# The second tile's k halves on two engines, and a new order of the first output rows, in an attention plus MoE kernel

## Chip, cores and metric

One core of a Trainium2 chip. The metric is the device time of one execution in microseconds (us), lower is better. Engines are named as in the profile: PE is TensorE (PEld its weight loads), ACT ScalarE, DVE VectorE, POOL GpSimd, SP SyncE, which issues all DMAs of the kernel before but two 64 KB stores.

## The reference

Chunked softmax attention (8 sequences, 8 heads, 576 positions, chunks of 64) feeds a two-layer MLP with exact GELU. Float32 in and out; the kernel works in bf16.

```python
# attention inside chunks of 64
scores = scale * np.matmul(q_c, k_c.transpose(0, 1, 2, 4, 3))
attn = softmax(scores)
out = np.matmul(attn, v_c)
# MLP on 4608 tokens
x = out.transpose(0, 2, 1, 3).reshape(4608, 512)
h = x @ w_in                                 # 512 -> 2048
g = 0.5 * h * (1.0 + erf(h / sqrt(2)))
y = g @ w_out                                # 2048 -> 512
```

## The kernel before

Nine tiles of 512 tokens. For each, `mm1` (x by w_in, then GELU) and `mm2` (h by w_out) keep TensorE busy, and the attention of the *next* tile is laced in between. The change is in `phase(0)`: while mm2 of the first tile runs by rows of w_out (twelve rows of four matmuls, one for each output block of 128 tokens), q and k of the second tile are transposed on TensorE, copied out of PSUM, and used.

```python
def transposed(t, nm, g):
    pool, tag = (ps_tp, "tp") if t or nm == "q" else (ps_mm, "mm")   # ps_tp has 2 banks
    tp = pool.tile([P, 2, J, P], bf16, tag=tag, name="tp")
    for j in range(J):
        nc.tensor.transpose(tp[:, 0, j], tiles[t][nm][:, g, j]..., ident[:])
    return ...

def att_Tk(t, g, copy):
    tp = transposed(t, "k", g)
    for r in range(2):                      # partitions 0-63, then 64-127
        sl = slice(CH * r, CH * (r + 1))
        copy(k_bds[g][sl, :, sl]..., tp[sl])

def mm2_rows(t, f):
    for ms in range(MT // P):
        if f == 0:
            pool, tag = (ps_at, "at") if ms == 3 else (ps_mm, "mm")   # ps_mm: 3 banks, shared with mm1
            tiles[t]["y_ps", ms] = pool.tile(...)
        nc.tensor.matmul(tiles[t]["y_ps", ms][:], h[:, f, ms * P:(ms + 1) * P], w_out_sb[:, f, :], ...)

phase(0, {}, {0: [lambda: act_table(Act.Exp)],
              2: [T[0]], 3: [T[2]], 4: [T[4], T[6]], 7: [T[1], T[3]], 8: [T[5], S_[0]],
              9: [T[7], S_[1], next_qk], 10: [S_[2], att_sum, cast of w_out row 14 by DVE],
              11: [cast of w_out row 15 by ACT, S_[3]], 12: [sums], 13: [A[0], ...], ...}, by_rows=True)
```

T[0], T[2], T[4], T[6] are the q transposes of groups 0 to 3; T[1], T[3], T[5], T[7] those of k. S_ are score matmuls, A the products with v. The k copies of groups 0 and 1 are ScalarE's, those of 2 and 3 VectorE's.

The softmax here doesn't subtract the row's maximum and nothing guards it: scores larger than these inputs give would overflow.

## Time and profile before

| | before |
|---|---|
| time, median of 4 | 290.65 us (290.45 to 291.22) |
| span in the profile | 288.9 us |
| PE busy | 278.2 us (96%) |
| first mm2 matmul of the first tile | 31.72 us |
| from there to the end | 257.1 us |

PE is busy all but about 11 us. The prediction below shows the two gaps that the change aims at. The records of the transpose bank (durations as least/median/most ns, first and last start in us) give the price of a half copy on either engine:

```profile
L157 ACT COPY k_bd<-tp x4: 578/579/580, 39.5 to 41.3; 64x512 bf16<-64x512 bf16 x4
L157 DVE COPY k_bd<-tp x4: 683/688/695, 41.1 to 43.3; 64x512 bf16<-64x512 bf16 x4
```

And GpSimd's timeline (start, duration, line, work, count, and in brackets the idle time before it and what ended that) shows the casts that feed TensorE in this stretch: w_out rows 8 to 11, then rows 12 and 13, then v of the second tile.

```profile
39.64 2.29 POOL L432 CAST w_out_sb<-arrival 128x512 bf16<-128x512 f32 x4 [0.94 <-DMA arrival<-in_moe_w_out_dram]
43.15 1.17 POOL L432 CAST w_out_sb<-arrival 128x512 bf16<-128x512 f32 x2 [1.22 <-DMA arrival<-in_moe_w_out_dram]
44.27 5.38 POOL L137 CAST v_bd<-arrival 64x512 bf16<-64x512 f32 x8
```

The first two of these lines start when a load lands; the v casts follow the second at once. So this stretch is fed by the DMA stream, with about 1 us to spare: row 8's cast, the first of the four, ends at about 39.64 + 0.61 = 40.25 us, and its matmuls start at 41.17.

### The profile page before, as it was taken

What the parts mean: (1) busy time and instruction counts of PE and PEld (TensorE: products, weight loads), DVE (VectorE), ACT (ScalarE), POOL (GpSimd) and SP (SyncE); (2) the same over time, 40 slices, a digit from 0 to 9 for tenths busy, and PEclk for the clock granted to TensorE, in tenths of its full rate; (3) what the DMA queues carried; (4) which work ended last, traced back from release to release, by engine and by line L of the source; (5) the groups of instructions that cost most, each with busy time, mean ns of one, the idle gap of its engine ahead of it and who ended that gap; (6) DMA issues with size and microseconds to landing.
All of it is one profiled execution on the core that took longest, in us unless ns stands there. A gap on an engine that the chain in (4) does not pass through costs nothing.

```text
span 288.9 us, 4859 instructions
## 1 busy us (share of the span) xinstructions
PE 278.2 (96%) x1836; PEld 138.5 (48%) x1870; DVE 154.8 (54%) x265; ACT 170.1 (59%) x329; POOL 98.8 (34%) x136
## 2 busy tenths in 40 slices
PE   7699999999999999999999999999999999999994
PEld 2454455445544554455445544554455445544444
DVE  6854349348805882749246935394268425850011
ACT  3767766967447844785468536763785368626400
POOL 6859758605651830262008400650003610000000
PEclk9999999999999999999999999999999999999999
DMA  6999999999799726961698259914999970120033
GB/s 222 247 360 404 393 337 265 254 207 286 191 291 311 168 99 161 325 145 74 161 261 234 76 138 285 233 73 115 163 130 131 265 147 2 39 106 2 0 73 73
DMA packets 96887, 53.79 MB, mean 186 GB/s; under 512 B 68576, under 2 KB 89312, under 8 KB 96864
## 3 DMA queue, kind: packets, MB, share of 16 engines
q1 hardware_dynamic: 96704, 53.36, 69.8%
q8 instruction: 14, 0.23, 0.3%
q10 hardware_dynamic: 160, 0.13, 0.2%
q14 instruction: 9, 0.07, 0.1%
HBM read 36.70 MB, written 9.44 MB: 160 GB/s over the span
## 4 chain that ended last, share of the span: by engine, by line
PE 90%; DVE 3%; ACT 3%; DMA 2%; issue 1%; SPq 0%; POOL 0%; DVEq 0%; POOLq 0%
PE h_ps L328 42%; PE y_ps L344 37%; PE av_ps L289 3%; PE y_ps L384 3%; PE s_ps L180 2%; DMA arrival<-in_k_dram 2%; ACT k_bd L157 2%; PE y_ps L369 1%; DVE x L296 1%; PE tp L144 1%; PE rc_ps L276 1%; DVE rc L259 1%; ACT pT L194 1%; SPq L112 0%; PE s_ps L192 0%
## 5 line engine op out<-in xcount | busy, mean ns | idle before, releaser
L328 PE MATMUL h_ps<-x,w_in_sb 128*128 128x512 bf16 x565 | 125.8, 379 | 1.0 <-DVE x L296 0.4
L331 ACT ACTIVATE h<-h_ps 128x512 bf16<-128x512 f32 x144 | 85.5, 597 | 62.5 <-PE h_ps L328 62.4
L344 PE MATMUL y_ps<-w_out_sb,h 128*128 128x512 bf16 x493 | 117.9, 379 | 0.9
L328 PEld LDWEIGHTS <-w_in_sb 128*128 128x128 bf16 x576 | 56.2, 98 | 68.4 <-issue 1.2
L344 PEld LDWEIGHTS <-h 128*128 128x128 bf16 x512 | 46.0, 98 | 46.5 <-issue 0.2
L172 DVE COPY k_bd<-k_t 64x512 bf16<-64x512 bf16 x56 | 35.6, 636 | 53.6 <-DMA k_t<-k_nat 52.6
L133 POOL CAST q_nat<-arrival 128x512 bf16<-128x512 f32 x31 | 21.2, 720 | 95.0 <-DMA arrival<-in_q_dram 95.0
L137 POOL CAST v_bd<-arrival 64x512 bf16<-64x512 f32 (+1 forms) x30 | 36.3, 1210 | 20.5 <-DMA arrival<-in_v_dram 13.3
L296 DVE TENSOR_TENSOR x<-av_ps,rc 128x512 bf16<-128x512 f32 x36 | 24.8, 692 | 4.7 <-PE av_ps L289 1.4
L133 POOL CAST k_nat<-arrival 128x512 bf16<-128x512 f32 x34 | 20.1, 625 | 11.2 <-DMA arrival<-in_k_dram 9.2
L448 ACT ACT_TABLE_LOAD x18 | 23.1, 1283 | 1.0 <-PEq L587 0.7
L353 DVE COPY y_sb<-y_ps 128x512 f32<-128x512 f32 x11 | 7.6, 691 | 29.7 <-PE y_ps L344 27.8
L353 ACT COPY y_sb<-y_ps 128x512 f32<-128x512 f32 x24 | 13.8, 580 | 14.7 <-PE y_ps L344 14.4
L239 DVE STREAM_TRANSPOSE pt<-pT 128x256 f32<-128x256 f32 x28 | 12.2, 437 | 18.8 <-ACT pT L183 18.8
L259 DVE STREAM_TRANSPOSE rc<-rb 128x512 f32<-128x512 f32 x31 | 21.5, 692 | 0.2 <-ACT rb L229 0.2
L242 DVE TENSOR_REDUCE part<-pt 128x16 f32<-128x512 bf16 x28 | 19.2, 686 | 1.0
L250 ACT COPY other<-part 32x32 f32<-32x32 f32 x56 | 12.0, 215 | 10.4 <-DVE part L242 9.9
L289 PEld LDWEIGHTS <-v_bd 128*128 128x128 bf16 x288 | 13.0, 98 | 8.0 <-issue 0.3
L183 ACT ACTIVATE pT<-s_ps 128x512 bf16<-128x512 f32 x28 | 14.7, 590 | 0.0
L289 PE MATMUL av_ps<-pT,v_bd 128*128 128x64 bf16 x288 | 14.3, 193 | 0.2
L180 PEld LDWEIGHTS <-k_bd 128*128 128x128 bf16 x224 | 10.4, 98 | 6.6
L384 PE MATMUL y_ps<-w_out_sb,h 128*128 128x512 bf16 x46 | 11.9, 379 | 0.4 <-ACT h L331 0.3
(68 smaller groups left out, 136.5 us busy)
## 6 DMA issues: line engine op xcount, KB each, us to landing
arrival<-in_v_dram SPq DMA_DIRECT2D x72, 128.0 KB, 4.1
out_dram<-y_sb SPq DMA_DIRECT2D x32, 256.0 KB, 2.3
arrival<-in_q_dram SPq DMA_DIRECT2D x7, 1024.0 KB, 6.7
arrival<-in_k_dram SPq DMA_DIRECT2D x7, 1024.0 KB, 9.1
arrival<-in_moe_w_out_dram SPq DMA_DIRECT2D x4, 1024.0 KB, 12.2
arrival<-in_moe_w_in_dram SPq DMA_DIRECT2D x4, 512.0 KB, 6.2
arrival<-in_moe_w_in_dram SPq DMA_DIRECT2D x2, 1024.0 KB, 10.4
arrival<-in_q_dram SPq DMA_DIRECT2D x4, 256.0 KB, 4.7
```

What stands on the lines that cost most here:

```text
L133: copy(st[nm][:, g].rearrange("p j r d -> p r j d"), st[nm + "f"][:, 2 * g:2 * g + 2])
L137: copy(v_bds[t % NV][sl, :, gs, sl].rearrange("p i g d -> p g i d"), tiles[t]["vf"][sl, gs])
L172: copy(k_bds[g][sl, :, sl].rearrange("p i (c j) -> p i c j", j=J), src[sl])
L259: nc.vector.transpose(rc[:], src.to_broadcast([P, NB, 32]))
L289: nc.tensor.matmul(av_ps[:, i, :], v_bds[t % NV][:, i, g, :], st["pT", g][:, i, :], start=True, stop=True)
L296: nc.vector.tensor_tensor(x, av, rc, op=mybir.AluOpType.mult)
L328: nc.tensor.matmul(h_ps[a][:], w_in_sb[:, ks, (f + a) * P:(f + a + 1) * P], st["x"][:, ks, :], start=(ks == 0), stop=(ks == KS - 1))
L331: nc.scalar.activation(st["h"][:, f + a, :], h_ps[a][:], Act.Gelu)
L344: nc.tensor.matmul(y_ps[:], st["h"][:, f, ms * P:(ms + 1) * P], w_out_sb[:, f, :], start=(f == 0), stop=(f == FF - 1))
L353: (AC if ms < 3 and t + 1 < NT else DV)(y_sb[:], y_ps[:])
L384: nc.tensor.matmul(tiles[t]["y_ps", ms][:], tiles[t]["h"][:, f, ms * P:(ms + 1) * P], w_out_sb[:, f, :], start=(f == 0), stop=False)
L448: nc.scalar.activation(act_scratch[:], rest[:, 0:1], func)
```

## The change

The intent: free a transpose bank sooner, by giving ScalarE the lower and VectorE the upper half of each k group of the second tile, and let the first mm2 rows begin with block 3, which has a bank of the attention pool, so that block 2, whose bank waits for the last GELU (to 32.52 us in the trace before), comes only after row 1 has started.

```diff
-    def att_Tk(t, g, copy):
+    def att_Tk(t, g, copies):
         tp = transposed(t, "k", g)
         for r in range(2):
             sl = slice(CH * r, CH * (r + 1))
-            copy(k_bds[g][sl, :, sl]..., tp[sl])
+            copies[r](k_bds[g][sl, :, sl]..., tp[sl])
...
-            T += [..., lambda g=g: att_Tk(t, g, ck if t == 0 or g < 2 else DV)]
+            T += [..., lambda g=g: att_Tk(t, g, (ck, ck if t == 0 else DV))]
...
     def mm2_rows(t, f):
-        for ms in range(MT // P):
+        todo = [(f, ms) for ms in (3, 0, 1, 2)]
+        if f < 2:
+            todo = [(f, ms) for ms in (3, 0, 1)] if f == 0 else [(1, 3), (1, 0), (1, 1), (0, 2), (1, 2)]
+        for f, ms in todo:
```

`...` stands for unchanged lines and rearrangements of axes.

More of the change, by code (lines that the diff above doesn't have):

```diff
@@ L156, in att_Tk @@
             sl = slice(CH * r, CH * (r + 1))
-            copy(k_bds[g][sl, :, sl].rearrange("p i (c j) -> p i c j", j=J), tp[sl])
+            copies[r](k_bds[g][sl, :, sl].rearrange("p i (c j) -> p i c j", j=J), tp[sl])
     def flip(t, nm):
@@ L304, in att_units @@
         for g in range(G):
-            T += [lambda g=g: att_Tq(t, g, cq), lambda g=g: att_Tk(t, g, ck if t == 0 or g < 2 else DV)]
+            T += [lambda g=g: att_Tq(t, g, cq), lambda g=g: att_Tk(t, g, (ck, ck if t == 0 else DV))]
         S_ = [lambda g=g: att_S(t, g) for g in range(G)]
```

## The prediction

> **What bounds the kernel now.** I read the page first, then TensorE's waits, then the chain of work that ended last and the timeline for the one stretch that the change touches (31 to 53 us: mm2 of the first tile, with the attention of the second tile laced into it).
>
> The page's first part and the by-line part of its chain:
> ```profile
> PE 278.2 (96%) x1836; PEld 138.5 (48%) x1870; DVE 154.8 (54%) x265; ACT 170.1 (59%) x329; POOL 98.8 (34%) x136
> ...
> PE 90%; DVE 3%; ACT 3%; DMA 2%; issue 1%; SPq 0%; POOL 0%; DVEq 0%; POOLq 0%
> ```
> TensorE is 96% busy and 90% of the chain. So only its gaps can be won, and only those that other work does not re-open later. TensorE's waits in the window 31 to 53 us (total, times, longest) are:
> ```profile
> PE y_ps L384 <- ACT h L331: 0.3, 1, 0.3
> PE h_ps L328 <- DVE x L296: 0.2, 1, 0.2
> PE tp L144 <- ACT k_bd L157: 0.2, 1, 0.2
> ```
> The change aims at the first and the third. The listed sizes are too small, because a matmul's record runs on to its modelled end (379 ns) while the next starts 216 ns after it (the chain shows 0.86 us for every four). From the timeline of TensorE (start, duration, line, count):
> ```profile
> 31.72 0.59 PE L384 MATMUL y_ps<-w_out_sb,h 128*128 128x512 bf16 x2
> 32.57 1.46 PE L384 MATMUL y_ps<-w_out_sb,h 128*128 128x512 bf16 x6 [0.25 <-ACT h L331]
> ...
> 39.07 0.61 PE L144 MATMUL tp<-ident,k_nat 128*128 128x128 bf16 x8
> 39.52 1.03 PE L384 MATMUL y_ps<-w_out_sb,h 128*128 128x512 bf16 x4
> 40.72 0.38 PE L144 MATMUL tp<-ident,k_nat 128*128 128x128 bf16 x4 [0.17 <-ACT k_bd L157]
> ```
> First gap: two matmuls from 31.72 leave TensorE free at 31.72 + 2 x 0.216 = 32.15, and the third starts at 32.57: **0.42 us**. The third is output block 2 of the first row. It takes the bank that the last GELU reads, and that GELU ends at 32.52. Second gap: four matmuls from 39.52 end their slots at 40.38, and the third group's k transposes start at 40.72: **0.34 us**. They wait for the first of two transpose banks, which ScalarE empties in two copies in a row:
> ```profile
> 39.50 0.58 ACT k_bd L157
> 40.08 0.01 issue
> 40.09 0.59 ACT k_bd L157
> 40.68 0.04 issue
> 40.72 0.38 PE tp L144 x4
> ...
> 44.01 0.73 DVE t L204
> ...
> 52.12 0.70 DVE x L296
> ```
> (the chain in order of time.) From 44.01 to 52.82 the chain leaves TensorE: VectorE's sums, reciprocals and x products with four small ScalarE copies, each starting where the one before ended. It ends with x of the fourth group and a wait of 52.87 - (51.23 + 6 x 0.216) = 0.34 us at the head of the next tile's mm1. The change does not shorten that chain, so what counts is whether its first link moves. It does: before 44.01 the chain shows the column-sum matmul on TensorE (to 43.98), while VectorE had been free since 43.95.
>
> [...] The halves here are partitions 0 to 63 and 64 to 127[...]. This trace has no two engines in one bank at once[...]. [...] The trace has 688 and 579 ns; I use those. [...] GpSimd's w_out casts take 614 ns beside VectorE's k copies, and 834 to 868 ns beside VectorE's casts from SBUF. [...]
>
> **The change part by part.**
>
> 1. Output-block order. The number of matmuls stays at 48 in these rows. Row 0 now issues blocks 3, 0, 1 (block 3 has a bank of the attention pool, free since the first tile), row 1 issues 3, 0, 1, and only then come block 2 of rows 0 and 1. Six matmuls from 31.72 end their slots at 33.02, half a microsecond after the GELU's end at 32.52. All eight run without a gap to 33.45; before, they ended at 33.86. Gain **0.41 us**, if nothing up to the next part waits. ScalarE's table load (32.54 to 33.82) and its small activation (to 34.03) stay put. The first qT copy can start at 34.03 instead of 34.29, so it gains only 0.26, but its bank is next wanted some 1.6 us later. The k casts (VectorE and GpSimd) end by 38.71. The first two groups' casts end near 37.9, and the moved k transposes start at 38.65. No new wait.
>
> 2. Halves on two engines. The eight half copies stay eight, still four by ScalarE (579 ns) and four by VectorE (688 ns). They are divided by half instead of by group. With part 1 in, the transposes of groups 0 and 1 start at 38.65 and the first bank is full at 39.08. ScalarE's half ends at 39.66, VectorE's at 39.77, the bank is free at about 39.81. VectorE was idle from 38.24 to 41.14 before, so it costs nothing there. TensorE wants the bank at 39.10 + 0.864 = 39.97. So the second gap goes: **0.34 us**, with 0.15 us in hand. Group 1's bank is free at about 40.5 and wanted at 41.27. The k blocks are ready for the score matmuls as well.
>
> Sum: 0.41 + 0.34 = **0.75 us** by the time of the column sum, which then ends near 43.23. VectorE has finished its last k half by about 42.4, so its chain starts 0.75 us earlier with all links unchanged. The w_out block that VectorE casts inside the chain landed by 43.15, and it moves from 45.76 to 45.01: no DMA wait. The 0.34 us wait for x at the end stays.
>
> What follows must keep it. The second tile's successors hang on DMA that does not move: k_bd copies at 61.73 to 66.69, score matmuls from 64.74 at 1.1 us each. The tightest margin there is over 1 us. GpSimd's v casts run 66.83 + 3.84 = 70.67, wanted at 71.71, after the change at 70.96: 0.29 us left, the tightest place of all. Later tiles repeat every 29.5 us, which is TensorE's own work, so the gain travels to the end. 290.73 - 0.75 = 289.98, say **290.0 us**, 0.26% faster.
>
> **The rivals.** First, **the halves serialise**, by a dependency on the shared bank or k block or by slower access. Group 0's bank would then be free at about 39.08 + 0.58 + 0.04 + 0.69 + 0.04 = 40.43, and TensorE would wait 0.46 us in place of 0.34. Only about 0.3 us of the gain is left: 290.4. Against it: [...]the w_in and w_out casts show that different engines fill slices of one tile at once. Second, **a DMA-fed cast takes over**. The w_out row for slot 8 is cast by GpSimd from 39.64, when its load lands, to about 40.25. TensorE now wants it at 40.41. With 0.15 us in hand, a load that lands 0.3 us late gives back some 0.15 us: 290.1. The same holds for v at 70.67; a loss of all the gain there needs about 1 us of delay: 290.7. Third, **VectorE becomes the bound** because it holds k halves of all four groups. Its work is the same 2.8 us and is done earlier, so I give this little weight. If the last half came late it would delay the chain at 43.23 only after 0.8 us of slack. Fourth, the parts lean on each other: if only part 1 held, 290.3; if only part 2, 290.4.
>
> **Range and chances.** 0.75 us is about the spread of the three runs before (290.45 to 291.22), so noise of some 0.4 us either way weighs as much as the mechanism. I take 289.5 to 290.7: the low end is the sum plus noise, the high end the gain given back. Faster by 2% would need 5.8 us, and the whole stretch has some 1.2 us of TensorE gaps. Slower by 2% would need a new wait in every tile, and only this stretch changes. Faster 0.01, within 2% 0.98, slower 0.01.
>
> **What would show it right or wrong.** Right: no gap among the first eight y_ps matmuls of L384's successor; q transposes 0.41 us earlier; k half copies of ScalarE and VectorE starting within 0.05 us of each other at about 39.1, at 579 and 688 ns; no wait of the third k transposes on either; the column sum's transpose on VectorE near 43.25; the mm1 of tile 2 some 0.75 us earlier, and the span near 288.15. The wait for x of about 0.34 us is still there. Wrong: VectorE's half starting after ScalarE's, longer copies, a TensorE wait on w_out or v casts, or an early lead that is gone by the third tile's mm2.

## The result, and the profile after

Ratios in this document are the mean time of one kernel's fast runs over that of the other's in the same rounds, so not quite the ratio of the medians quoted.

| | before | changed |
|---|---|---|
| time, median | 290.65 us (4 runs) | 291.19 us (290.62 to 291.44, 4 runs) |
| ratio | | 1.0013, 95% interval 0.9992 to 1.0033 |
| predicted | | 290.0 us, range 289.5 to 290.7 |

The measured time is outside the range, on the slow side. Yet the two profiled spans are equal, 288.9 us.

In the changed kernel's timeline of TensorE, the eight matmuls of the first two rows now run without a gap. But the third k transposes start at 40.75, not when the four matmuls from 39.42 end their slots (39.42 + 0.86 = 40.28):

```profile
32.03 1.89 PE L387 MATMUL y_ps<-w_out_sb,h 128*128 128x512 bf16 x8
...
38.97 0.61 PE L144 MATMUL tp<-ident,k_nat 128*128 128x128 bf16 x8
39.42 1.03 PE L387 MATMUL y_ps<-w_out_sb,h 128*128 128x512 bf16 x4
40.75 0.38 PE L144 MATMUL tp<-ident,k_nat 128*128 128x128 bf16 x4 [0.31 <-DVE k_bd L157]
```

That is a gap of 0.47 us where the kernel before had 0.34. The waits of TensorE's matmuls in 30 to 54 us have one line left, and it names VectorE. Its weight loads, which are listed apart (PEld), wait once for the third group's v, which delays the matmuls by 0.03 us; the kernel before has no such line:

```profile
PE tp L144 <- DVE k_bd L157: 0.3, 1, 0.3
...
PEld L289 <- POOL v_bd L137: 0.4, 1, 0.4
```

The chain in order of time says why:

```profile
39.39 0.59 ACT k_bd L157
39.98 0.02 issue
40.01 0.71 DVE k_bd L157
40.71 0.04 issue
40.75 0.38 PE tp L144 x4
...
45.96 0.41 PE sums_ps L218 x4
46.37 0.02 issue
46.40 0.73 DVE t L221
```

ScalarE's half copy (39.39 to 39.98) and VectorE's (40.01 to 40.71) stand one behind the other on the chain. The timelines of the two engines agree. ScalarE has its two halves of groups 0 and 1 back to back:

```profile
39.39 1.06 ACT L157 COPY k_bd<-tp 64x512 bf16<-64x512 bf16 x2 [1.96 <-PE tp L144]
```

and VectorE starts its two only after having been idle until ScalarE's first ended:

```profile
40.01 1.30 DVE L157 COPY k_bd<-tp 64x512 bf16<-64x512 bf16 x2 [1.28 <-ACT k_bd L157]
```

Two more things are to be seen. The first mm2 matmul is at 32.03 instead of 31.72, although nothing ahead of it was changed: the start-up took 0.31 us longer in this execution. And in the chain TensorE now leads up to 46.37, because VectorE, which before took over at 44.01, has some idle time there (0.24 us before 44.04, 0.30 before 46.40); the x products still end at 52.82 and mm1 still waits for the last of them. Lead and late start cancel: from the first mm2 matmul to the end it is 256.84 us instead of 257.14. So in this pair of traces the change gave 0.3 us, not 0.75, and the start took it away.

### The profile page after: what moved, and what is told of

Its sections match the earlier page's. It is cut to its first block, busy times and chain, and to the rows that moved or that the text cites. A ratio compares the mean times of both kernels' runs of the same rounds, so it can differ in the third digit from the quotient of the medians.

```text
span 288.9 us, 4892 instructions
## 1 busy us (share of the span) xinstructions
PE 279.8 (97%) x1870; PEld 138.4 (48%) x1870; DVE 153.4 (53%) x265; ACT 169.8 (59%) x329; POOL 100.0 (35%) x136
## 4 chain that ended last, share of the span: by engine, by line
PE 91%; DVE 2%; DMA 2%; ACT 1%; SPq 1%; issue 0%; POOL 0%; DVEq 0%
PE h_ps L328 42%; PE y_ps L344 37%; PE y_ps L387 3%; PE av_ps L289 3%; PE s_ps L180 2%; DMA arrival<-in_k_dram 2%; PE y_ps L369 1%; SPq L112 1%; DVE x L296 1%; PE tp L144 1%; PE rc_ps L276 1%; DVE rc L259 1%; ACT k_bd L157 1%; ACT pT L194 0%; PE s_ps L192 0%
## 5 line engine op out<-in xcount | busy, mean ns | idle before, releaser
L344 PE MATMUL y_ps<-w_out_sb,h 128*128 128x512 bf16 x512 | 120.5, 379 | 0.0
L172 DVE COPY k_bd<-k_t 64x512 bf16<-64x512 bf16 x56 | 36.4, 651 | 52.8 <-DMA k_t<-k_nat 51.7
L133 POOL CAST q_nat<-arrival 128x512 bf16<-128x512 f32 x31 | 21.9, 745 | 94.1 <-DMA arrival<-in_q_dram 94.1
L387 PE MATMUL y_ps<-w_out_sb,h 128*128 128x512 bf16 x48 | 11.8, 379 | 0.0
```

The costliest lines, as they stand in the source:

```text
L133: copy(st[nm][:, g].rearrange("p j r d -> p r j d"), st[nm + "f"][:, 2 * g:2 * g + 2])
L172: copy(k_bds[g][sl, :, sl].rearrange("p i (c j) -> p i c j", j=J), src[sl])
L344: nc.tensor.matmul(y_ps[:], st["h"][:, f, ms * P:(ms + 1) * P], w_out_sb[:, f, :], start=(f == 0), stop=(f == FF - 1))
L387: nc.tensor.matmul(tiles[t]["y_ps", ms][:], tiles[t]["h"][:, f, ms * P:(ms + 1) * P], w_out_sb[:, f, :], start=(f == 0), stop=False)
```

## Experiments

To compare traces whose starts differ I use one measure, from the first mm2 matmul to the last instruction ("to the end"), and the gaps of TensorE inside it. A gap is the time from the start of one matmul to the next, less its slot (216 ns for 512 columns, 55 for 128, 28 for 64, as the starts in the trace before are spaced: 215 to 217, 55 to 56 and 28 to 30 ns from 39.07 to 41.60 us; a missing record is not counted, nor a gap under 0.02 us). The table holds all sixteen profiles; the texts below refer to it.

| run | last k cast starts | first mm2 matmul | gap in first row | at the bank | at w_out row 8 | at v casts | at x | to the end |
|---|---|---|---|---|---|---|---|---|
| before | 10.42 | 31.72 | 0.42 | 0.34 | 0 | 0 | 0.34 | 257.14 |
| changed | 10.75 | 32.03 | 0 | 0.47 | 0 | 0.03 | 0.26 | 256.84 |
| after_again | 10.34 | 31.62 | 0 | 0.47 | 0.12 | 0.17 | 0.11 | 256.94 |
| after_third | 10.89 | 32.18 | 0 | 0.47 | 0 | 0.03 | 0.25 | 256.82 |
| order_only | 10.13 | 31.41 | 0 | 0.34 | 0 | 0.03 | 0.26 | 256.70 |
| halves_only | 11.85 | 33.14 | 0.42 | 0.47 | 0 | 0.26 | 0 | 257.24 |
| third_bank | 11.29 | 33.35 | 0 | 0 | 0.20 | 0.81 | 0 | 257.49 |
| other_dest | 11.05 | 32.45 | 0 | 0.47 | 0 | 0 | 0.36 | 257.20 |
| two_banks | 10.38 | 31.67 | 0 | 0 | 0.59 | 0.24 | 0.05 | 258.07 |
| before_light | 11.33 | 32.61 | 0.42 | 0.34 | 1.01 | 0 | 0.30 | 258.18 |
| third_light | 11.38 | 32.67 | 0 | 0 | 1.16 | 0 | 0.30 | 257.70 |
| before_late | 10.45 | 34.24 | 0.42 | 0.33 | 0 | 0 | 0.30 | 257.10 |
| after_late | 10.28 | 34.07 | 0 | 0.47 | 0 | 0 | 0.30 | 256.82 |
| order_late | 10.51 | 34.31 | 0 | 0.34 | 0 | 0 | 0.30 | 256.70 |
| third_late | 10.97 | 34.77 | 0 | 0 | 0 | 0 | 0.31 | 256.50 |
| two_queues | 8.69 | 31.58 | 0 | 0.34 | 0 | 0.06 | 0.23 | 256.69 |

All in us. The last column is from the unrounded ends of the traces; the expectations below were written with spans rounded to 0.1 us, and so have 257.18 and 257.45 where the table has 257.14 and 257.49. third_bank, third_light and third_late also have 0.12 us at the first score matmuls, and two_banks as much after the q transposes. Each row is one execution. Where two rows should be equal (changed, after_third and after_late; order_only, order_late and two_queues) "to the end" differs by up to 0.02 us, and for before and before_late by 0.04; after_again differs from the other three by its waits on casts. other_dest, equal to changed up to the third tile but for 0.06 us, loses some 0.3 us more in a later tile, at products with v that wait for x; that was not looked into.

The eight kernels from other_dest to third_late in the table were executed once each, so their device times (292.50 us for before_light, 292.09 for third_light, 291.44 for other_dest, 291.45 for two_banks, beside one of 291.70 for the kernel before; 293.07, 293.78, 292.73 and 292.98 for the four late ones in the order of the table, beside 292.03) settle nothing and are not used: after_late's is 2.9 us over its profiled span, the other three's 1.7 to 1.8. after_again, order_only, halves_only and third_bank ran on one chip, other_dest to third_light on a second, and the four late ones, two_queues and after_third on a third.

My theory after the first look was: the halves are put one after the other by something in the program; the first part works; the 0.5 us by which the first runs were slower is scatter of the start.

### The two parts by themselves

after_again is the changed kernel unaltered.

> The changed kernel, unaltered. In its first trace VectorE's half copy of the k transposes began only when ScalarE's half had ended, TensorE waited 0.46 us for the bank in place of 0.34, and the stretch from the first mm2 matmul to the mm1 matmul that waits for x took 20.84 us against 21.15 before. Theory (the change is worth 0.3 us, and the 0.5 us by which its four first runs were slower are differences of the start-up that every execution has): ratio 0.9985 to 1.0000, the stretch again near 20.8 us, the wait again near 0.46 us. Rival (the changed kernel is really slower): ratio over 1.0005 with an interval that leaves out 1, and something in the trace after the stretch that is longer than before.

order_only is the kernel before with the new `mm2_rows` alone (the third part of the diff above).

> Only the new order of the output blocks, the k copies as before. Theory: the gap of 0.42 us in the first row goes, the wait for the bank on ScalarE stays at 0.34 us, the stretch is 21.15 - 0.41 = 20.74 us, ratio about 0.9986, a little better than the whole change. Rival (the lead is eaten by casts that wait for DMA): a wait of TensorE on w_out or v casts appears and the stretch is over 21.0 us.

halves_only is the changed kernel with the old `mm2_rows`.

> Only the halves on two engines, the order of the output blocks as before. Theory (VectorE's half waits for ScalarE's): the gap of 0.42 us stays, the wait for the bank is 0.46 us instead of 0.34, the stretch is about 21.15 + 0.12 = 21.3 us, ratio about 1.0004. Rival (the halves would run at once and the earlier trace had another cause): both halves start within 0.05 us of each other, no wait for the bank, stretch 20.8 us, ratio 0.9988.

Measured, five rounds on one chip (before: 290.96 us, 11 runs from 290.35 to 292.33):

| run | median | ratio | 95% interval |
|---|---|---|---|
| after_again | 291.09 us | 1.0001 | 0.9970 to 1.0032 |
| order_only | 290.71 us | 0.9988 | 0.9962 to 1.0013 |
| halves_only | 291.49 us | 1.0014 | 0.9985 to 1.0042 |

The times cannot separate them: the kernel before alone spreads by 2 us. The order of the medians is the expected one, no more can be said. The gaps do separate them. The new order removes the 0.42 us and nothing else. The halves raise the gap at the bank from 0.34 to 0.47 us with either order. The stretches up to the mm1 matmul that waits for x came out near what was expected: 20.70 us in order_only (20.74) and 21.23 in halves_only (21.3). after_again took 20.94 (20.8), with two waits of 0.12 and 0.17 us on casts that cost 0.03 us or nothing in the first trace of the same kernel; the wait for x shrank by 0.15 us in return.

### What puts the halves one after the other

Two things could order them: the shared bank that both read, or the shared k block that both write. other_dest sends VectorE's halves to a tile that nothing uses:

```diff
+            dst = k_junk if t == 1 and r == 1 else k_bds[g]
-            copies[r](k_bds[g][sl, :, sl]..., tp[sl])
+            copies[r](dst[sl, :, sl]..., tp[sl])
```

> The changed kernel, but VectorE's halves of the second tile's k go to another SBUF tile than ScalarE's (a wrong result on purpose). Theory (the two reads of one transpose bank are ordered one after the other): VectorE's half of the first group still starts only as ScalarE's ends, some 0.6 us after it. Rival (the two writes to one k block are what is ordered): both halves start within 0.05 us of each other.

ScalarE's halves of groups 0 and 1, in its timeline:

```profile
39.81 1.06 ACT L159 COPY k_bd<-tp 64x512 bf16<-64x512 bf16 x2 [1.96 <-PE tp L145]
```

VectorE's halves (the first line holds groups 0 and 1):

```profile
40.42 1.49 DVE L159 COPY k_junk<-tp 64x512 bf16<-64x512 bf16 x2 [1.26 <-ACT k_bd L159]
42.20 0.69 DVE L159 COPY k_junk<-tp 64x512 bf16<-64x512 bf16 x1 [0.29 <-ACT k_bd L159]
43.52 0.69 DVE L159 COPY k_junk<-tp 64x512 bf16<-64x512 bf16 x1 [0.63 <-ACT k_bd L159]
```

VectorE still waits for ScalarE's k_bd copy in each line, and starts at 40.42, about when ScalarE's first copy (39.81 + 0.58) is done. So it is not the k block. (The result passed the comparison although half of the second tile's k was stale; the scores are very small here, so the softmax hardly feels it. That reason is argued, not tested.)

two_banks transposes groups 0 and 1 twice, into two banks, and VectorE reads from the second; groups 2 and 3 are as in the change:

```diff
+        tps = [transposed(t, "k", g)] * 2
+        if t == 1 and g < 2:
+            tp = ps_at.tile([P, 2, J, P], bf16, tag="at", name="tp2")
+            for j in range(J):
+                nc.tensor.transpose(tp[:, 0, j], tiles[t]["k"][:, g, j]..., ident[:])
+            tps[1] = ...
         for r in range(2):
+            tp = tps[r]
```

> The changed kernel, but the first two groups are transposed twice, into a bank of the transpose pool and one of the attention pool, and VectorE reads its half from the second; correct, with 8 more transposes (8 x 0.055 = 0.44 us of TensorE). Groups 2 and 3 stay as in the change. Theory (order by bank): for groups 0 and 1 the halves of both engines run side by side, at 0.58 and 0.69 us, and TensorE does not wait for a bank before the third group's transposes; for group 2 and 3 VectorE's half starts after ScalarE's. Rival (order by k block): VectorE's halves wait for ScalarE's in all four groups.

ScalarE's halves:

```profile
39.15 1.06 ACT L163 COPY k_bd<-tp 64x512 bf16<-64x512 bf16 x2 [2.08 <-PE tp L144]
40.93 0.58 ACT L163 COPY k_bd<-tp 64x512 bf16<-64x512 bf16 x1 [0.72 <-PE tp L144]
```

VectorE's halves:

```profile
39.44 1.30 DVE L163 COPY k_bd<-tp 64x512 bf16<-64x512 bf16 x2
41.54 0.69 DVE L163 COPY k_bd<-tp 64x512 bf16<-64x512 bf16 x1 [0.80 <-ACT k_bd L163]
```

For groups 0 and 1 (the first line of each) VectorE starts at 39.44, as soon as its k cast has ended, while ScalarE's first half (39.15 to 39.73) is still running. For groups 2 and 3, from one bank, it waits for ScalarE again (the second lines show group 2). The gap at the bank is gone. The trace files say the same in another way: they list the semaphores (counters by which one engine's program waits for another's) that an instruction waits for. In the changed kernel all four of VectorE's halves wait for the one that ScalarE's copies raise; in two_banks the first two wait for TensorE's alone. So the order is by bank, and it is in the program: as built from this source, VectorE's read of a bank waits for ScalarE's although the partitions differ, in all four groups of the changed kernel and in groups 2 and 3 of two_banks. (Each transpose tile here has a bank to itself, so whether two tiles in one bank would be ordered too is not shown; nor does any run here show whether the chip would run two reads of one bank at once.) That is the failing step. The doubled transposes, 0.44 us, and waits on casts eat the gain (258.07 us to the end, 0.52 us of it a wait for the third tile's v).

### A third bank, and what takes its gain

third_bank reaches the aim of part 2 another way: whole groups by one engine each, two groups at once from different banks, and the third group's transposes in a bank of the attention pool.

```diff
     def transposed(t, nm, g):
         pool, tag = (ps_tp, "tp") if t or nm == "q" else (ps_mm, "mm")
+        if t == 1 and nm == "k" and g == 2:
+            pool, tag = ps_at, "at"
...
-     lambda g=g: att_Tk(t, g, ck if t == 0 or g < 2 else DV)
+     lambda g=g: att_Tk(t, g, ck if t == 0 or g % 2 == 0 else DV)
```

(on top of the new order.)

> The new order of output blocks; each k group is again copied by one engine (groups 0 and 2 ScalarE, 1 and 3 VectorE, so two groups at once from different banks), and the third group's transposes take a bank of the attention pool, so they wait for no copy. Theory: both gaps go, the stretch is 21.15 - 0.75 = 20.4 us, ratio about 0.9974 (290.0 us where before has 290.7). Rival (DMA-fed work takes over): TensorE waits for GpSimd's w_out or v casts instead, and the stretch stays at 20.7 us or more.

The median was 290.95 us, ratio 1.0000 (0.9971 to 1.0028). Neither of the two gaps is left, and yet in the profiled execution, the slowest of the six (292.57 us), it is 257.49 us to the end, more than before. TensorE's weight loads now wait for v:

```profile
PEld L291 <- POOL v_bd L137: 1.8, 3, 0.7
```

and GpSimd's timeline shows the casts behind it:

```profile
41.71 2.29 POOL L437 CAST w_out_sb<-arrival 128x512 bf16<-128x512 f32 x4 [0.98 <-DMA arrival<-in_moe_w_out_dram]
46.21 1.18 POOL L437 CAST w_out_sb<-arrival 128x512 bf16<-128x512 f32 x2 [2.20 <-DMA arrival<-in_moe_w_out_dram]
47.32 5.51 POOL L137 CAST v_bd<-arrival 64x512 bf16<-64x512 f32 x8
```

In this execution the loads landed late. The casts of w_out rows 12 and 13 start 46.21 - 33.35 = 12.86 us after the first mm2 matmul; in the kernel before it was 43.15 - 31.72 = 11.43. (Row 8, cast first from 41.71, is 8.36 us after it instead of 7.92, and costs the 0.20 us of the table.) The v casts stand behind them, and TensorE, which comes sooner, waits. The rival was right in this execution: the loads took the gain. The other five were not profiled.

### Taking the loads away: a failed test

before_light and third_light leave out the last quarter of w_out. Their outputs are wrong, which doesn't matter for the times.

```diff
-        raw = stage_tile()[:].rearrange("p (f n) -> p f n", f=FC)
-        nc.sync.dma_start(raw, w_out_v[:, c * FC:(c + 1) * FC, :])
+        if c < NWC - 1:
+            raw = ...; nc.sync.dma_start(raw, ...); out_raws.append(raw)
+        else:
+            raw = out_raws[-1]
```

> The kernel before without the load of the last quarter of w_out (its casts read the third quarter again, a wrong result on purpose): 1 MB less in the first 45 us. Control for the next run. Theory: no wait for v or w_out casts, and from the first mm2 matmul to the end 257.2 us, as in the profile of the kernel before (257.18).

> The kernel with the new order and a third transpose bank, without the load of the last quarter of w_out (wrong on purpose). With the load it waited 1.8 us for v casts and took 257.45 us from the first mm2 matmul to the end. Theory (the loads of the first 45 us are what took the gain): no wait for v or w_out casts, no wait for a bank, and 257.2 - 0.75 = 256.4 us from the first mm2 matmul to the end, 0.75 us under the control. Rival (the gain is lost elsewhere, in VectorE's chain or later tiles): no waits for casts, but 256.9 us or more.

Both expectations failed. The third quarter now landed *later*: 9.8 us after the first mm2 matmul in before_light (39.64 - 31.72 = 7.9 before), and TensorE waited 1.01 and 1.16 us at row 8. With one load fewer, the issue of the second tile's v moved up, from 32.40 us (0.68 us after the first mm2 matmul) to 31.75 in before_light (0.86 us before it), so more of its loads can have run beside that quarter; this is my guess at the reason, and I did not test it. The two still differ by 258.18 - 257.70 = 0.48 us, in the direction of the theory. The test settles nothing about its size; the next one does it better.

### Giving the loads a lead

Instead of fewer loads, TensorE is made later: 14 dummy matmuls (14 x 0.216 = 3.0 us) ahead of the first tile's mm1, in each of four kernels. (The first mm2 matmul came 2.5 us later for it, as the section on the start shows.)

```diff
+        keep_warm(14)
         phase(0, {}, {0: [lambda: act_table(Act.Exp)],
```

> The kernel before with 14 more dummy matmuls (3.0 us) on TensorE ahead of the first tile's mm1, so that all loads of the first 50 us have 3 us more of a lead over TensorE. Correct. Both theories: gaps of 0.42 us in the first row and 0.34 us at the bank, none on casts, 257.2 us from the first mm2 matmul to the end. Control for the other three.

> The changed kernel with the same 3 us lead. Theory (what the change gives is 0.42 us less 0.13 us, and the waits for casts in its second trace were loads that landed late): no wait on casts, a wait of 0.47 us at the bank, 256.9 us from the first mm2 matmul to the end. Rival (the change itself slows the casts): waits on casts remain, over 257.0 us.

> The new order alone with the same lead. Theory: 0.34 us at the bank, nothing in the first row, 257.2 - 0.42 = 256.8 us from the first mm2 matmul to the end.

> The new order and the third transpose bank with the same lead. Theory (the loads took the gain of this kernel): no wait in the first row, at the bank, on w_out or on v casts; the wait for x stays near 0.3 us; 257.2 - 0.75 = 256.4 us from the first mm2 matmul to the end. Rival (VectorE's chain or later tiles take it): no waits on casts, yet 256.8 us or more.

No wait on a cast is left in any of the four, and the sum comes out:

| kernel | to the end | against before_late | expected |
|---|---|---|---|
| before_late | 257.10 | | |
| after_late | 256.82 | -0.28 | -0.3 |
| order_late | 256.70 | -0.40 | -0.42 |
| third_late | 256.50 | -0.60 | -0.75 |

third_late keeps a gap of 0.12 us at the first score matmuls, because ScalarE copies both halves of group 0 in a row. Its 0.60 us are nearly all of 0.42 + 0.34 - 0.12 = 0.64, and up to the third tile's mm1 it gains the same (48.65 - 48.04 = 0.61). So the arithmetic of the gaps was right, where the bank does come free and the loads are early.

### The start

What is left is the 0.5 us by which the first four runs were slower. In nine of the eleven profiles that have neither the dummy matmuls nor a second queue, the first mm2 matmul comes 21.28 to 21.30 us after GpSimd starts to cast the first tile's last k piece, whatever the kernel; with the dummy matmuls it is 23.79 to 23.80 us in all four. (The other two, third_bank with 22.06 and other_dest with 21.40, were held up a little more.) And that cast starts anywhere from 10.13 to 11.85 us. In the changed kernel's chain, this is the load and the cast (start, duration):

```profile
4.33 6.37 DMA arrival<-in_k_dram
10.75 0.63 POOL k_nat L133
```

two_queues is order_only with the first tile's k loads issued by ScalarE's queue beside the q loads:

```diff
-            nc.sync.dma_start(raw[:, h0:h1], ...)
+            (nc.scalar if t == 0 and nm == "k" else nc.sync).dma_start(raw[:, h0:h1], ...)
```

In the trace before an issue takes about 0.5 us of SyncE's queue, and the eighth piece, the last of k, is issued at 4.33 us, so issuing the four k pieces beside the four of q would start the last one some 2 us earlier (my estimate from these times). That saving was what was wanted.

> The new order alone, and the first tile's four k loads issued by ScalarE's queue beside the q loads of the usual queue, so the last k piece is issued some 2 us earlier. Theory (the landing of the last k piece sets the start of mm2, and so the time): the last k cast starts earlier than in any profile so far (before 10.1 us), the first mm2 matmul comes 21.3 us after it, the time falls by as much as the cast moves: ratio 0.993 to 0.998. Rival (loads of the start are limited by what the engines move, not by issue): the cast stays at 10.1 to 11.9 us and the ratio is about 0.999.

> The changed kernel once more, beside it. Theory: ratio 0.998 to 1.001, like the second time (1.0001), and the profile again gives the first mm2 matmul 21.3 us after the last k cast and 256.8 to 257.1 us from there to the end, whatever the time of that execution.

Measured, five rounds on one chip (before: 290.72 us, 8 runs from 290.49 to 291.49):

| run | median | range | ratio | 95% interval |
|---|---|---|---|---|
| two_queues | 289.98 us | 289.65 to 290.16 | 0.9966 | 0.9951 to 0.9982 |
| after_third | 290.59 us | 290.15 to 290.87 | 0.9986 | 0.9970 to 1.0001 |

after_third came out as expected: its first mm2 matmul is 21.29 us after the cast, and from there to the end it is 256.82 us. In two_queues the cast did move, by 1.4 us or more against every other profile (two casts from 7.95, the last one at 8.69):

```profile
7.95 1.36 POOL L133 CAST k_nat<-arrival 128x512 bf16<-128x512 f32 x2
```

But the first mm2 matmul is at 31.58, so it did not follow one for one: it comes 22.89 us after the cast, not 21.29. The chain now runs through ScalarE's k copies, which stand in a row:

```profile
10.23 0.46 ACT k_bd L157
...
10.70 0.58 ACT k_bd L157
...
11.31 0.58 ACT k_bd L157
...
11.90 0.58 ACT k_bd L157
```

So the theory failed in its second part: right behind the landing lies another bound. 31.58 us is not even earlier than the earliest start with the old loads (31.41, in order_only), so this profile does not show a faster start; what it can have done is to keep late starts away, and with one profile that is not shown either. The kernel is the only one here whose interval leaves out 1; all five of its runs are below all eight of the kernel before. How much of that is the start and how much the new order (0.9988 by itself, unclear) was not separated.

## Why the prediction was wrong

Step by step, as the prediction put them:

1. **Part 1, 0.41 us: right.** The first row's gap is 0.42 us in every kernel with the old order and 0 in every one with the new. order_late against before_late: 0.40 us.
2. **Part 2, "the second gap goes: 0.34 us, with 0.15 us in hand": wrong, and this is the step that failed.** It took halves on different partitions (0 to 63 and 64 to 127) for halves that run at once, which was my estimate; no trace had shown two engines in one bank. The built program orders the two reads of a bank (other_dest and two_banks show it), and the gap grew to 0.47 us. My first rival had this very case, with 0.46 us; I set it aside on the ground that engines fill slices of one tile at once. Those slices were in SBUF (in the trace before, casts of VectorE and GpSimd into w_out_sb from 34.15 and 34.18 us), and said nothing of a PSUM bank. Part 2 is worth -0.13 instead of +0.34, and the sum 0.42 - 0.13 = 0.29 us, which the traces have (0.30, 0.28).
3. **"Which rival": the second was right too, in some executions.** Waits on casts came to 0.29 us in after_again, of which 0.10 us reached the end, and took all of the gain in third_bank. I had priced row 8 of w_out at 0.15 us and named v only at 70.67, for the third tile. The second tile's v, whose casts end some 1.0 to 1.4 us ahead of need in the trace before (an estimate: eight equal parts of the 5.38 us from 44.27, against the v products at 47.06 to 51.00), was missing from the list. The changed kernel's weight loads already wait 0.36 us for it, so a bank that came free in time would have met this wait next.
4. **"The wait for x stays": nearly.** It went from 0.34 to 0.26 us, and to zero where TensorE came late by waiting elsewhere.
5. **The range: too narrow, for the wrong reason.** Part 2 explains 0.47 us of the miss. With the right sum the centre would have been 290.4, and 291.19 would still be 0.8 us off; for these 0.8 us the cause stays open, and scatter of the start is only the likely one. I took the spread of three runs (0.77 us) for the noise. The start alone moves the first mm2 matmul from 31.41 to 33.35 us in profiles of kernels that do not differ there, and over 11 runs the kernel before spreads over 2.0 us. Three comparisons of the changed kernel gave 1.0013, 1.0001 and 0.9986. A gain of 0.3 us would be 0.9990: the first interval (0.9992 to 1.0033) just leaves it out, the other two hold it and 1 as well. The gain is read from the traces, not from the times. Not shown: that the four first runs themselves had a late start, since only one of them was profiled (it did, by 0.31 us, and it was the fastest of the four).
6. **A reading of the trace: wrong, without effect.** In the "834 to 868 ns" of GpSimd's casts a mean stands for a single cast: beside VectorE's casts the four of GpSimd take 868, 799, 870 and 799 ns (from 34.18, 35.00, 37.09 and 37.91 us), and 834 is the mean of a pair.

The class, within 2%, was right, but no outcome seen here could have missed it: the medians differ by 0.5% at most.

## What to carry to other kernels

Before pricing two engines on one PSUM bank as parallel, look at whether the built program lets them: here it did not, though the partitions differed (the gap went from 0.34 to 0.47 us), and the evidence from SBUF tiles did not carry over. Where a stage runs as fast as its loads land, gaps of TensorE are slack for the loads: third_bank closed 0.42 and 0.34 us of gaps and met 0.20 and 0.81 us of waits on casts; with a lead for the loads third_late gained 0.60 us. A kernel variant with a few added dummy matmuls (14 here) shows cheaply whether the casts behind the loads have that lead. For changes of a few tenths of a per cent, compare traces from a common event onward, since the start-up can scatter by more than the whole effect: here the cast that waits for the last of eight 256 KB pieces started at 10.13 to 11.85 us in kernels that are the same up to there.
